# Fewer accumulating DMAs for the weighted values, two new ones for the second half's products, and another split of the last output tiles

## The chip, the cores and the metric

The kernel runs on one core of a Trainium2 chip. The metric is the device time of one execution in microseconds: the median of three runs was 166.25 us, between 166.01 and 166.59.

## What is computed

Two branches read the same input of 2048 tokens by 512 channels (bfloat16), and a gate for each token mixes them. The first is an attention of 32 heads of 16 channels, in which a token sees itself and seven earlier tokens at a distance of 2, 4, ... 14. The second is an MLP over the tokens: the normalised input is multiplied by w1 (2048 x 1792), passed through a gelu and multiplied by w2 (1792 x 2048).

```
g = sigmoid((x * gate_w).sum(-1))
logits[s, w] = (q[s] . k[s - 2 w]) / 4          # w = 0..7, masked where s - 2w < 0
o[s] = sum over w of softmax(logits)[s, w] * v[s - 2 w]
a = o @ wo
b = (w2^T gelu(w1^T layernorm(x) + b1) + b2)    # over the token axis
out = g * a + (1 - g) * b
```

## The kernel before

**Stages on TensorE.** The projections to q, k and v (L667, up to 50.4 us) come first. The MLP's first product, `ph2`, has 14 blocks of 128 hidden units (L582; 16 matmuls each, and 14 for the first four blocks, whose first two input tiles are done early at L591). Then comes the second product, `ph3`, for 16 output tiles of 128 tokens (L855; 14 matmuls of 512 columns each, in two halves). To each tile's sums the attention's projection `wo` is added in the same PSUM bank (L864; four matmuls). `wo` of a tile runs five tiles behind its `ph3`, and the last five tiles' `wo` come at the end, together with that of tile 15, which is cut into pieces by columns.

**The attention's logits.** Channels are laid out so that a group of four channels of each head ("head-dim" `dl` = 0..3) forms one layer of 128 partitions. For a half `h` of 1024 tokens VectorE multiplies q and the eight shifted copies of k, one layer at a time (`qk`, L755 to 761; 128x8192 elements for all eight distances), and adds the four products (`qadd`, L763). Buffers P0, P1 and P2 hold 128x8192 bfloat16 each; a fourth lies over the logits' space. TensorE then sums the channels of each head with 16 matmuls of 32 columns (`sum0`, `sum1`, L747), ScalarE copies the logits out (`lev`), and VectorE and ScalarE do the softmax (L784 to 799): maxima, subtraction, `exp`, three sums (`sm4`, `sm2`, `sm1`), a logarithm (`lns`), an addition (`rsz`), an exponential (`rb`) and a multiplication (`nrm`). ScalarE loads another function table between these and the gelus that stand among them in its order.

In the first half the product of layer 1 is added to that of layer 0 by an accumulating DMA that GpSimd issues (`qd0`, L769, 2 MB). In the second half VectorE does all: `qk(0)`, then for layers 1 to 3 a product into P1 and an addition to P0.

**Weighted values.** GpSimd copies the weights to all four layers (`av0_*`, `av1_*`, L809, 16 DMAs of 128 KB for each half). For each of eight units `u` of 256 tokens VectorE multiplies the weights with v (`avm`, L820, 128x8192), and the eight distances are added in three steps: 8 to 4, 4 to 2 (`avb`) and 2 to 1 (`avc`, which writes what `wo` of tiles 2u and 2u+1 reads). The first step is an accumulating DMA of 1 MB on GpSimd's queue (`avd`, L823) for the units in the list `AVD` (L30: 1 to 6) and a VectorE addition of 128x4096 (`ava`, L827) for units 0 and 7.

**The end.** ScalarE scales a finished tile from PSUM to SBUF (`ev`, L875) and SP writes it out (`d_out`, L877). Tile 15 is cut at columns 256 and 384 (L896): VectorE evacuates the first and the last piece (L911), ScalarE the second; SP writes VectorE's two, ScalarE's queue its own.

**Order.** Each operation is recorded with its engine, an assumed duration, a priority and the names of the buffers that it reads and writes (`_Sched.add`). A list scheduler (L125 to 222) gives each engine a fixed order by assumed times; semaphore waits are then planned from the buffer names (L224). Thus an edit in one place can move instructions of any engine. On TensorE most of the order is chained by hand (`PE`, L550), and the two `sum` operations are put in by priority. SP issues the loads in its own fixed order: weights of `ph2` come in seven loads `w1_0` to `w1_6` of two blocks each (three buffers; a load waits until the blocks that used its buffer are done), the weights of `ph3` in eight loads `w2_0` to `w2_7`, which reuse space of other buffers: `w2_2` goes into P2 and waits until P2 is free (`W2ALIAS`, L368).

`PR` (L370) gives the resource names of the four product buffers.

```
        PR = [["p0"], ["p1"], ["p2", "p2h"], ["log0", "log1", "att0", "att1", "lw"]]
```

Of the kernel before, what the change touches and what calls it, by code (L numbers as in the profile page):

```python
# [8 lines left out]
ALU = mybir.AluOpType  # L9
AF = mybir.ActivationFunctionType  # L10
# [3 lines left out]
D = 512  # L14
# [4 lines left out]
NST = S // 128  # L19
NFT = F // 128  # L20
PAD = 14
HS = S // 2
KR = HS + PAD
# [3 lines left out]
ZMAX = 60.0  # L27
NOELIDE = False
NLEAD = 2
AVD = (1, 2, 3, 4, 5, 6)  # L30
GL = 4


# [272 lines left out]
def bass_gated_mix__sliding_local_dilated__mixer_token_mlp__prompt_kernel(nc, A_x, A_wqkv, A_wo, B_x, B_w1, B_b1, B_w2, B_b2, gate_w, out, dbg=None):  # L306
    with contextlib.ExitStack() as es:
# [45 lines left out]
        outv = out[0].rearrange("(t p) d -> p t d", p=128)  # L353
# [7 lines left out]
        def w2view(name, extra=0):  # L361
# [5 lines left out]
               w2view("X"), w2view("X", NFT * 256)]  # L367
        W2ALIAS = [XTALL, XTALL, ["p2"], ["w1s1"], ["w1s2"], ["w1s0"],  # L368
                   ["x%d" % t for t in range(7)], ["x%d" % t for t in range(7, 14)]]
        PR = [["p0"], ["p1"], ["p2", "p2h"], ["log0", "log1", "att0", "att1", "lw"]]  # L370
        LW = view("LOG", BF16, [(128 * GL, NLEAD), (1, 128 * GL)])
        WO = view("WO", BF16, [(D, 4), (1, D)])
        QH = [view("Q%d" % h, BF16, [(HS, 4), (1, HS)]) for h in range(2)]
        KH = [view("K%d" % h, BF16, [(KR, 4), (1, KR)]) for h in range(2)]
        V5 = view("V5", BF16, [(VR, 4), (1, VR)])
        PB = [view(b, BF16, [(HS, NW), (1, HS)]) for b in ("P0", "P1", "P2", "LOG")]
# [4 lines left out]
        OT = view("OT", BF16, [(4 * UT_, 8), (UT_, 4), (1, UT_)])  # L381
        OTRES = ["log0", "log0", "log1", "log1", "att0", "att0", "att1", "att1"]
# [10 lines left out]
        OUTS = view("OUTS", BF16, [(D, 5), (1, D)])  # L393
# [32 lines left out]
        OMG = small(NST)  # L426
        C2 = small(NST)
# [4 lines left out]
        def col(v_, i):  # L432
            return bass.AP(v_.tensor, v_.offset + i, [list(v_.ap[0]), [1, 1]])
# [4 lines left out]
        def sub(ap_, offs, dims):  # L438
            return bass.AP(ap_.tensor, ap_.offset + offs, [list(ap_.ap[0])] + [list(d) for d in dims])
# [5 lines left out]
        def tt(o_, a_, b_, op_):  # L445
            return lambda e: e.tensor_tensor(out=o_, in0=a_, in1=b_, op=op_)  # L446

        def act(o_, i_, f_, **kw):
            return lambda e: e.activation(out=o_, in_=i_, func=f_, **kw)  # L449
# [170 lines left out]
        r0 = rstd(0)  # L620
# [5 lines left out]
        r1 = rstd(1)  # L626
# [65 lines left out]
        for dl in range(4):  # L692
# [3 lines left out]
          reads=["k%d_1" % dl for dl in range(4)], writes=["khalo"], name="khalo")  # L696
# [8 lines left out]
        for dl in range(4):  # L705
            for sb in range(4):
                proj(2, dl, sb)
            if dl == 0:
                te = bank_()

                def f_te(e):
# [6 lines left out]
                  reads=["b%d" % te], writes=["e1"], name="e1", prio=-30)  # L718
# [4 lines left out]
        for t in range(NLEAD, NST):  # L723
            A("dve", (lambda t_: lambda e: e.bn_stats(out=ST6[:, t_, :], in_=X[:, t_, :]))(t), 0.67,  # L724
              reads=["x%d" % t], writes=["st%d" % t], after=[e3], name="st%d" % t, prio=-4)
# [28 lines left out]
        for h in range(2):  # L754
            def qk(dl, b_):  # L755
                for s_, n_ in (((0, 512), (512, 512)) if h == 0 else ((0, HS),)):
                    sbs = [2 * h + x_ for x_ in range(s_ // 512, (s_ + n_) // 512)]
                    A("dve", tt(sub(PB[b_], s_, [(HS, NW), (1, n_)]), sub(QH[h], dl * HS + s_, [(0, NW), (1, n_)]),
                                sub(KH[h], dl * KR + PAD + s_, [(-2, NW), (1, n_)]), ALU.mult), 4.32 * n_ / HS + 0.1,
                      reads=["q%d_%d" % (dl, x_) for x_ in sbs] + ["k%d_%d" % (dl, x_) for x_ in sbs] + (["khalo"] if h else ["kpad"] if s_ == 0 else ["k%d_0" % dl]),  # L760
                      writes=PR[b_], name="qk%d_%d_%d" % (h, dl, s_))

            def qadd(a_, b_):  # L763
                A("dve", tt(PB[a_], PB[a_], PB[b_], ALU.add), 4.42, reads=PR[b_], writes=PR[a_], name="qa%d_%d" % (h, a_))
            if h == 0:
                qk(0, 0)
                qk(1, 1)
                rows = [(2048, 4), (1, 2048)]
                sch.dma("pool", (lambda d_, s_: lambda e: e.dma_start(d_, s_, accum_op=ALU.add, max_dma_last_dim=4096))(sub(PB[0], 0, rows), sub(PB[1], 0, rows)),  # L769
                        int(3.2e6), sch.dsem("qd%d" % h), issue=1.0, reads=PR[1], writes=PR[0], name="qd%d" % h)  # L770
                qk(2, 2)
                qk(3, 3)
                qadd(2, 3)
                qadd(2, 0)
                fin = 2
            else:
                qk(0, 0)
                for dl in range(1, 4):
                    qk(dl, 1)
                    qadd(0, 1)  # L780
                fin = 0
            A("pe", f_sum(fin), 1.0, reads=PR[fin] + ["rp"], writes=LGB, name="sum%d" % h, prio=-100, delay=0.5)
            A("act", act(LOG[h], ps[:, 4:8, :], AF.Copy), 1.9, reads=LGB, writes=["log%d" % h], name="lev%d" % h, prio=-5)
            if h == 0:  # L784
# [30 lines left out]
        for u in range(8):  # L815
            h, c = u // 4, u % 4
            b = 1 if u % 2 == 0 else 0
            pv = PV[b]
            vr = ["v%d_%d" % (dl, sb) for dl in range(4) for sb in sorted(set([u // 2, max(0, (256 * u - PAD)) // 512]))]
            A("dve", tt(pv, sub(V5, PAD + 256 * u, [(-2, NW), (VR, 4), (1, UT_)]), sub(AVW[h], c * NW * UT_, [(UT_, NW), (0, 4), (1, UT_)]), ALU.mult), 4.42,  # L820
              reads=["avw%d_%d_%d" % (h, c, dhi) for dhi in range(4)] + vr + ["vpad"], writes=["p%d" % b], name="avm%d" % u)
            if u in AVD:
                sch.dma("pool", (lambda d_, s_: lambda e: e.dma_start(d_, s_, accum_op=ALU.add, max_dma_last_dim=4096))(  # L823
                    sub(PB[b], 0, [(2048, 2), (1, 2048)]), sub(PB[b], 4096, [(2048, 2), (1, 2048)])),
                    int(1.6e6), sch.dsem("avd%d" % u), issue=1.0, writes=["p%d" % b], name="avd%d" % u)
            else:
                A("dve", tt(pv[:, 0:4], pv[:, 0:4], pv[:, 4:8], ALU.add), 2.28, writes=["p%d" % b], name="ava%d" % u)  # L827
            A("dve", tt(pv[:, 0:2], pv[:, 0:2], pv[:, 2:4], ALU.add), 1.22, writes=["p%d" % b], name="avb%d" % u)
            avl = A("dve", tt(OT[:, u], pv[:, 0], pv[:, 1], ALU.add), 0.68, reads=["p%d" % b], writes=["ot%d" % u, OTRES[u]], name="avc%d" % u)


        ring[0], ring[1] = 0, [0, 1, 2, 3]
# [34 lines left out]
            return fn  # L867

        ds_out = [sch.dsem("out%d" % k_) for k_ in range(4)]
        ds_last = [sch.dsem("outl%d" % k_) for k_ in range(3)]  # L870

        def finish_tile(i):
            bank = banks[i]
            PE(f_wo(i, bank, 0, D), 0.87, ["ot%d" % (i // 2), "wo"], ["b%d" % bank], "wo%d" % i)
            A("act", act(OUTS[:, i % 4, :], ps[:, bank, :], AF.Identity, scale=col(OMG, i), bias=col(C2, i)), 0.78,  # L875
              reads=["b%d" % bank, "omg", "c2"], writes=["outs%d" % (i % 4)] + (["p2h"] if i == 0 else []), name="ev%d" % i)
# [13 lines left out]
        for i in range(3, L):  # L890
            ph3(i, 0)
            ph3(i, 1)
            if i >= LAG:
                finish_tile(i - LAG)
        lastb = [bank_(), bank_(), bank_()]
        CH = ((0, 256), (256, 384), (384, 512))  # L896
        for hf, (c0, c1) in enumerate(CH):
            for half in range(2):
                PE(f_ph3(L, lastb[hf], half, c0, c1), 1.52 * (c1 - c0) / D, ["ut%d" % ft for ft in range(7 * half, 7 * half + 7)] + ["w2_%d" % (L // 2)],
# [3 lines left out]
        for hf, (c0, c1) in enumerate(CH):  # L903
            bank = lastb[hf]
            n_ = c1 - c0
            PE(f_wo(L, bank, c0, c1), 0.87 * n_ / D, ["ot%d" % (L // 2), "wo"], ["b%d" % bank], "wo%d_%d" % (L, hf))
            if hf == 1:
                A("act", act(OUTS[:, 4, c0:c1], ps[:, bank, 0:n_], AF.Identity, scale=col(OMG, L), bias=col(C2, L)), 0.4,
                  reads=["b%d" % bank, "omg", "c2"], writes=["outl%d" % hf], name="ev%d_%d" % (L, hf))
            else:  # L910
                A("dve", (lambda bank_, a_, b_: lambda e: e.tensor_scalar(out=OUTS[:, 4, a_:b_], in0=ps[:, bank_, 0:b_ - a_], scalar1=col(OMG, L),  # L911
                                                                          scalar2=col(C2, L), op0=ALU.mult, op1=ALU.add))(bank, c0, c1), 0.55 if hf == 0 else 0.4,
                  reads=["b%d" % bank, "omg", "c2"], writes=["outl%d" % hf], name="ev%d_%d" % (L, hf))
            sch.dma("act" if hf == 1 else "sp", (lambda a_, b_: lambda e: e.dma_start(outv[:, L, a_:b_], OUTS[:, 4, a_:b_]))(c0, c1), 256 * n_,
                    ds_last[hf], issue=0.5, reads=["outl%d" % hf], name="d_out%d_%d" % (L, hf))

        est = sch.schedule()
# [73 lines left out]
```

## Time and profile before

| | us |
|---|---|
| median of three runs | 166.25 (166.01 to 166.59) |
| the profiled execution | 165.4 |
| its span, first to last instruction | 164.1 |
| TensorE busy | 160.7 |
| VectorE busy | 143.1 |
| ScalarE busy | 77.0 |
| GpSimd busy | 26.8 |

The profile is of one execution. Its times are in microseconds from the start of the span, and lines such as L855 are those of the kernel. "PE" is TensorE, "DVE" VectorE, "ACT" ScalarE, "POOL" GpSimd and "SP" the engine that issues most DMAs; a "q" behind the name is the issue of a DMA. The granted TensorE clock was full throughout. Queue q1 holds the DMAs that SP issues, q0 those of GpSimd. A share of DMA engines over 100% comes from packets that overlap.

### The profile page before, as it was taken

What the parts mean: (1) busy time and instruction counts of PE and PEld (TensorE: products, weight loads), DVE (VectorE), ACT (ScalarE), POOL (GpSimd) and SP (SyncE); (2) the same over time, 40 slices, a digit from 0 to 9 for tenths busy, and PEclk for the clock granted to TensorE, in tenths of its full rate; (3) what the DMA queues carried; (4) which work ended last, traced back from release to release, by engine and by line L of the source; (5) the groups of instructions that cost most, each with busy time, mean ns of one, the idle gap of its engine ahead of it and who ended that gap; (6) DMA issues with size and microseconds to landing.
All of it is one profiled execution on the core that took longest, in us unless ns stands there. A gap on an engine that the chain in (4) does not pass through costs nothing.

```text
span 164.1 us, 2044 instructions
## 1 busy us (share of the span) xinstructions
PE 160.7 (98%) x819; PEld 76.8 (47%) x819; DVE 143.1 (87%) x113; ACT 77.0 (47%) x108; POOL 26.8 (16%) x61
## 2 busy tenths in 40 slices
PE   7999999999999999999999999999999999999994
PEld 3455555545554444444444444444444444444742
DVE  2939999999999999999999999999749294699992
ACT  3466776777776639849211977100121111111164
POOL 3000030000000000000693003087270302002000
PEclk9999999999999999999999999999999999999999
DMA  5999999999503899844898869999999997956914
GB/s 168 301 261 249 242 321 279 212 215 274 175 0 110 237 327 282 228 142 115 235 261 256 279 187 270 269 213 371 227 238 211 210 204 162 213 136 115 207 60 131
DMA packets 45150, 35.26 MB, mean 215 GB/s; under 512 B 7893, under 2 KB 41941, under 8 KB 45141
## 3 DMA queue, kind: packets, MB, share of 16 engines
q1 hardware_dynamic: 40960, 22.25, 49.9%
q0 software_dynamic: 3696, 12.59, 36.0%
q10 hardware_dynamic: 484, 0.30, 0.6%
q8 instruction: 6, 0.10, 0.2%
q14 instruction: 4, 0.02, 0.0%
HBM read 18.88 MB, written 2.10 MB: 128 GB/s over the span
## 4 chain that ended last, share of the span: by engine, by line
PE 95%; DMA 2%; DVE 1%; SPq 0%; issue 0%
PE ps L855 29%; PE ps L582 29%; PE ps L667 25%; PE ps L864 8%; DMA arena<-in_A_x_dram 2%; PE ps L747 1%; PE ps L591 1%; PE ps L684 1%; DVE arena L911 1%; SPq L483 0%; PE ps L559 0%; PE ps L714 0%; PE ps L574 0%; PE ps L576 0%; PE ps L575 0%
## 5 line engine op out<-in xcount | busy, mean ns | idle before, releaser
L446 DVE TENSOR_TENSOR arena<-arena 128x8192 bf16<-128x8192 bf16 (+9 forms) x67 | 125.4, 1905 | 14.1 <-DMA arena<-arena 10.1
L449 ACT ACTIVATE arena<-ps,arena 128x512 bf16<-128x512 f32 (+1 forms) x30 | 21.6, 725 | 61.1 <-PE ps L864 45.0
L855 PE MATMUL ps<-arena 128*128 128x512 bf16 (+2 forms) x252 | 50.2, 355 | 0.0
L582 PE MATMUL ps<-arena 128*128 128x512 bf16 x216 | 47.1, 379 | 0.0
L449 ACT ACTIVATE arena<-ps 128x512 bf16<-128x512 f32 (+3 forms) x53 | 34.2, 645 | 16.8 <-PE ps L667 14.0
L667 PE MATMUL ps<-arena 128*128 128x512 bf16 x192 | 42.0, 379 | 0.0
L855 PEld LDWEIGHTS ps<-arena 128*128 128x128 bf16 x252 | 23.6, 98 | 25.2
L582 PEld LDWEIGHTS ps<-arena 128*128 128x128 bf16 x216 | 21.0, 98 | 25.8 <-issue 0.8
L667 PEld LDWEIGHTS ps<-arena 128*128 128x128 bf16 x192 | 21.6, 113 | 19.7 <-ACT arena L449 0.4
L809 POOL DMA_DIRECT2D arena<-arena x32 | 17.6, 678 | 61.9 <-DVE arena L446 61.9
L864 PE MATMUL ps<-arena 128*128 128x512 bf16 (+2 forms) x72 | 15.8, 356 | 0.0
L940 ACT ACT_TABLE_LOAD x11 | 14.1, 1283 | 2.9 <-issue 2.7
L823 POOL DMA_DIRECT2D arena<-arena x6 | 7.3, 1220 | 39.6 <-DVE arena L446 39.6
L864 PEld LDWEIGHTS ps<-arena 128*128 128x128 bf16 x72 | 6.6, 98 | 7.5 <-DVE arena L446 0.8
L449 ACT ACTIVATE arena<-arena 128x1 f32<-128x1 f32 (+6 forms) x14 | 7.6, 544 | 4.2 <-DVE arena L446 3.6
L724 DVE BATCH_NORM_STATS2 arena<-arena 128x6 f32<-128x512 bf16 x14 | 8.7, 681 | 0.0
L769 POOL DMA_DIRECT2D arena<-arena x1 | 1.4, 1421 | 19.8 <-DVE arena L446 19.8
L737 DVE TENSOR_SCALAR arena<-arena 128x512 bf16<-128x512 bf16 x14 | 4.6, 407 | 0.0
L544 PE MATMUL ps<-const-bfloat16-1.0 128*128 128x512 bf16 x8 | 3.5, 569 | 0.9 <-PEq L976 0.9
L596 DVE BATCH_NORM_STATS2 arena<-arena 128x6 f32<-128x512 bf16 x2 | 1.4, 694 | 1.6 <-DMA arena<-in_A_x_dram 1.6
L911 DVE TENSOR_SCALAR arena<-ps,arena 128x256 bf16<-128x256 f32 (+1 forms) x2 | 0.9, 473 | 1.6 <-PE ps L864 1.6
L747 PE MATMUL ps<-arena 128*32 128x512 bf16 x32 | 2.1, 382 | 0.0
(37 smaller groups left out, 15.9 us busy)
## 6 DMA issues: line engine op xcount, KB each, us to landing
arena<-in_B_w_dram SPq DMA_DIRECT2D x10, 896.0 KB, 6.7
arena<-arena POOLq DMA_DIRECT2D x6, 1024.0 KB, 10.2
arena<-in_B_w_dram SPq DMA_DIRECT2D x5, 1024.0 KB, 6.8
arena<-arena POOLq DMA_DIRECT2D x32, 128.0 KB, 6.1
arena<-arena POOLq DMA_DIRECT2D x1, 2048.0 KB, 17.8
out_dram<-arena SPq DMA_DIRECT2D x15, 128.0 KB, 4.5
arena<-in_A_wqkv_dram SPq DMA_DIRECT2D x3, 512.0 KB, 5.8
arena<-in_A_x_dram SPq DMA_DIRECT2D x3, 512.0 KB, 4.8
```

The costliest lines, as they stand in the source:

```text
L446: return lambda e: e.tensor_tensor(out=o_, in0=a_, in1=b_, op=op_)
L449: return lambda e: e.activation(out=o_, in_=i_, func=f_, **kw)
L582: ins = e.matmul(ps[:, bank, :], lhsT=W1W[:, (ft // 2) % 3, st, 128 * (ft % 2):128 * (ft % 2) + 128], rhs=X[:, st, :], start=(st == 0), st ...
L667: ins = e.matmul(ps[:, bank, :], lhsT=sub(WQKV, dt * 3 * D + tn * D + dl, [(4, 128)]), rhs=XT[:, dt, sb * 512:(sb + 1) * 512], start=(dt = ...
L724: A("dve", (lambda t_: lambda e: e.bn_stats(out=ST6[:, t_, :], in_=X[:, t_, :]))(t), 0.67, reads=["x%d" % t], writes=["st%d" % t], after=[ ...
L737: A("dve", (lambda t_: lambda e: e.tensor_scalar(out=X[:, t_, :], in0=X[:, t_, :], scalar1=col(MS, t_), scalar2=col(RSTD2, t_), op0=ALU.su ...
L747: ins = e.matmul(ps[32 * c:32 * c + 32, 4 + wp, :], lhsT=RP, rhs=sub(PB[b_], 2 * wp * HS + c * UT_, [(HS, 2), (1, UT_)]), start=True, stop ...
L809: prev = sch.dma("pool", (lambda d_, s_: lambda e: e.dma_start(d_, s_))(dst, src), 131072, ds, issue=1.0, reads=["att%d" % h], writes=["av ...
L823: sch.dma("pool", (lambda d_, s_: lambda e: e.dma_start(d_, s_, accum_op=ALU.add, max_dma_last_dim=4096))(sub(PB[b], 0, [(2048, 2), (1, 20 ...
L855: ins = e.matmul(ps[:, bank, 0:c1 - c0], lhsT=W2S[i // 2][:, ft, 128 * (i % 2):128 * (i % 2) + 128], rhs=UT[:, ft, c0:c1], start=(ft == 0) ...
L864: ins = e.matmul(ps[:, bank, 0:c1 - c0], lhsT=OT[:, i // 2, dl, 128 * (i % 2):128 * (i % 2) + 128], rhs=WO[:, dl, c0:c1], start=False, sto ...
L940: e.preload_act_table_set(want)
```

## The change

It has four parts in the source.

1. `AVD` becomes 1, 3, 5: in units 2, 4 and 6 VectorE does the first addition.
2. In the second half, layers 0 and 1 are multiplied in two halves of four distances each (`qkw`, 128x4096), into P0 and P1; after each half of layer 1 a DMA of 1 MB (`qd1_0`, `qd1_4`) adds P1's half to P0's. Layer 2 is multiplied into P2, layer 3, again in two halves, into P1 as its halves come free, then P1 and P0 are added to P2. The sum is now in P2. P0 and P1 have two resource names each, one for each half.
3. Tile 14 is evacuated by VectorE.
4. Tile 15 is cut into two pieces, at column 288: the first is evacuated by ScalarE and written by its queue, the second by VectorE and SP.

```diff
-AVD = (1, 2, 3, 4, 5, 6)
+AVD = (1, 3, 5)
...
-        PR = [["p0"], ["p1"], ["p2", "p2h"], ["log0", "log1", "att0", "att1", "lw"]]
+        PR = [["p0", "p0b"], ["p1", "p1b"], ["p2", "p2h"], ["log0", "log1", "att0", "att1", "lw"]]
...
+            def qkw(dl, b_, w0):
+                A("dve", tt(sub(PB[b_], w0 * HS, [(HS, 4), (1, HS)]), sub(QH[h], dl * HS, [(0, 4), (1, HS)]),
+                            sub(KH[h], dl * KR + PAD - 2 * w0, [(-2, 4), (1, HS)]), ALU.mult), 2.25,
+                  reads=["%s%d_%d" % (c_, dl, 2 * h + x_) for c_ in "qk" for x_ in range(2)] + ["khalo"],
+                  writes=PR[b_][w0 // 4:w0 // 4 + 1], name="qk%d_%d_w%d" % (h, dl, w0))
...
+            def qd(b0, n_, nm, nb):
+                rows = [(2048, n_), (1, 2048)]
+                r0, r1 = (PR[0], PR[1]) if n_ == 4 else (PR[0][b0:b0 + 1], PR[1][b0:b0 + 1])
+                sch.dma("pool", (lambda d_, s_: lambda e: e.dma_start(d_, s_, accum_op=ALU.add, max_dma_last_dim=4096))(sub(PB[0], 4096 * b0, rows), sub(PB[1], 4096 * b0, rows)),
+                        nb, sch.dsem(nm), issue=1.0, reads=r1, writes=r0, name=nm)
...
             else:
-                qk(0, 0)
-                for dl in range(1, 4):
-                    qk(dl, 1)
-                    qadd(0, 1)
-                fin = 0
+                for w0 in (0, 4):
+                    qkw(0, 0, w0)
+                    qkw(1, 1, w0)
+                    qd(w0 // 4, 2, "qd1_%d" % w0, int(2.2e6))
+                qk(2, 2)
+                qkw(3, 1, 0)
+                qkw(3, 1, 4)
+                qadd(2, 1)
+            qadd(2, 0)
+            fin = 2
...
+        def ev_dve(i, o, bank, c0, c1, dur, res):
+            A("dve", lambda e: e.tensor_scalar(out=OUTS[:, o, c0:c1], in0=ps[:, bank, 0:c1 - c0], scalar1=col(OMG, i), scalar2=col(C2, i),
+                                               op0=ALU.mult, op1=ALU.add), dur, reads=["b%d" % bank, "omg", "c2"], writes=[res], name="ev%d_%d" % (i, c0))
...
+            if i == NST - 2:
+                ev_dve(i, i % 4, bank, 0, D, 0.75, "outs%d" % (i % 4))
+            else:
...
-        lastb = [bank_(), bank_(), bank_()]
-        CH = ((0, 256), (256, 384), (384, 512))
+        lastb = [bank_(), bank_()]
+        CH = ((0, 288), (288, 512))
```

The order that the scheduler then makes differs in these places. On TensorE `sum1` stands 16 matmuls of `ph2` earlier. On VectorE the second half's three half products come before the first half's softmax, the fourth after `msub0`; unit 1 is multiplied before unit 0, and unit 3 before unit 2. On SP `w2_2`, whose space is P2, is issued after `sum1` and not after `sum0`, behind `w2_3`. On ScalarE `lns1` comes before the last gelu.

More of the change, by code (lines that the diff above doesn't have):

```diff
@@ L767, in bass_gated_mix__sliding_local_dilated__mixer_token_mlp__prompt_kernel @@
                 qk(1, 1)
-                rows = [(2048, 4), (1, 2048)]
-                sch.dma("pool", (lambda d_, s_: lambda e: e.dma_start(d_, s_, accum_op=ALU.add, max_dma_last_dim=4096))(sub(PB[0], 0, rows), sub(PB[1], 0, rows)),
-                        int(3.2e6), sch.dsem("qd%d" % h), issue=1.0, reads=PR[1], writes=PR[0], name="qd%d" % h)
+                qd(0, 4, "qd0", int(3.2e6))
                 qk(2, 2)
@@ L773, in bass_gated_mix__sliding_local_dilated__mixer_token_mlp__prompt_kernel @@
                 qadd(2, 3)
-                qadd(2, 0)
-                fin = 2
-            else:
-                qk(0, 0)
-                for dl in range(1, 4):
-                    qk(dl, 1)
-                    qadd(0, 1)
-                fin = 0
+            else:
+                for w0 in (0, 4):
[8 more added lines that the diff above has]
+            fin = 2
             A("pe", f_sum(fin), 1.0, reads=PR[fin] + ["rp"], writes=LGB, name="sum%d" % h, prio=-100, delay=0.5)
@@ L820, in bass_gated_mix__sliding_local_dilated__mixer_token_mlp__prompt_kernel @@
             A("dve", tt(pv, sub(V5, PAD + 256 * u, [(-2, NW), (VR, 4), (1, UT_)]), sub(AVW[h], c * NW * UT_, [(UT_, NW), (0, 4), (1, UT_)]), ALU.mult), 4.42,
-              reads=["avw%d_%d_%d" % (h, c, dhi) for dhi in range(4)] + vr + ["vpad"], writes=["p%d" % b], name="avm%d" % u)
+              reads=["avw%d_%d_%d" % (h, c, dhi) for dhi in range(4)] + vr + ["vpad"], writes=PR[b], name="avm%d" % u)
             if u in AVD:
@@ L824, in bass_gated_mix__sliding_local_dilated__mixer_token_mlp__prompt_kernel @@
                     sub(PB[b], 0, [(2048, 2), (1, 2048)]), sub(PB[b], 4096, [(2048, 2), (1, 2048)])),
-                    int(1.6e6), sch.dsem("avd%d" % u), issue=1.0, writes=["p%d" % b], name="avd%d" % u)
+                    int(1.6e6), sch.dsem("avd%d" % u), issue=1.0, writes=PR[b], name="avd%d" % u)
             else:
-                A("dve", tt(pv[:, 0:4], pv[:, 0:4], pv[:, 4:8], ALU.add), 2.28, writes=["p%d" % b], name="ava%d" % u)
-            A("dve", tt(pv[:, 0:2], pv[:, 0:2], pv[:, 2:4], ALU.add), 1.22, writes=["p%d" % b], name="avb%d" % u)
-            avl = A("dve", tt(OT[:, u], pv[:, 0], pv[:, 1], ALU.add), 0.68, reads=["p%d" % b], writes=["ot%d" % u, OTRES[u]], name="avc%d" % u)
+                A("dve", tt(pv[:, 0:4], pv[:, 0:4], pv[:, 4:8], ALU.add), 2.28, writes=PR[b], name="ava%d" % u)
+            A("dve", tt(pv[:, 0:2], pv[:, 0:2], pv[:, 2:4], ALU.add), 1.22, writes=PR[b], name="avb%d" % u)
+            avl = A("dve", tt(OT[:, u], pv[:, 0], pv[:, 1], ALU.add), 0.68, reads=PR[b], writes=["ot%d" % u, OTRES[u]], name="avc%d" % u)
         ring[0], ring[1] = 0, [0, 1, 2, 3]
@@ L869, in bass_gated_mix__sliding_local_dilated__mixer_token_mlp__prompt_kernel @@
         ds_out = [sch.dsem("out%d" % k_) for k_ in range(4)]
-        ds_last = [sch.dsem("outl%d" % k_) for k_ in range(3)]
+        ds_last = [sch.dsem("outl%d" % k_) for k_ in range(2)]
+        def ev_dve(i, o, bank, c0, c1, dur, res):
+            A("dve", lambda e: e.tensor_scalar(out=OUTS[:, o, c0:c1], in0=ps[:, bank, 0:c1 - c0], scalar1=col(OMG, i), scalar2=col(C2, i),
+                                               op0=ALU.mult, op1=ALU.add), dur, reads=["b%d" % bank, "omg", "c2"], writes=[res], name="ev%d_%d" % (i, c0))
         def finish_tile(i):
@@ L874, in finish_tile @@
             PE(f_wo(i, bank, 0, D), 0.87, ["ot%d" % (i // 2), "wo"], ["b%d" % bank], "wo%d" % i)
-            A("act", act(OUTS[:, i % 4, :], ps[:, bank, :], AF.Identity, scale=col(OMG, i), bias=col(C2, i)), 0.78,
-              reads=["b%d" % bank, "omg", "c2"], writes=["outs%d" % (i % 4)] + (["p2h"] if i == 0 else []), name="ev%d" % i)
+            if i == NST - 2:
+                ev_dve(i, i % 4, bank, 0, D, 0.75, "outs%d" % (i % 4))
+            else:
+                A("act", act(OUTS[:, i % 4, :], ps[:, bank, :], AF.Identity, scale=col(OMG, i), bias=col(C2, i)), 0.78,
+                  reads=["b%d" % bank, "omg", "c2"], writes=["outs%d" % (i % 4)] + (["p2h"] if i == 0 else []), name="ev%d" % i)
             sch.dma("sp", (lambda i_: lambda e: e.dma_start(outv[:, i_, :], OUTS[:, i_ % 4, :]))(i), 131072, ds_out[i % 4], issue=0.5,
@@ L906, in bass_gated_mix__sliding_local_dilated__mixer_token_mlp__prompt_kernel @@
             PE(f_wo(L, bank, c0, c1), 0.87 * n_ / D, ["ot%d" % (L // 2), "wo"], ["b%d" % bank], "wo%d_%d" % (L, hf))
-            if hf == 1:
+            if hf == 0:
                 A("act", act(OUTS[:, 4, c0:c1], ps[:, bank, 0:n_], AF.Identity, scale=col(OMG, L), bias=col(C2, L)), 0.4,
-                  reads=["b%d" % bank, "omg", "c2"], writes=["outl%d" % hf], name="ev%d_%d" % (L, hf))
+                  reads=["b%d" % bank, "omg", "c2"], writes=["outl%d" % hf], name="ev%d_%d" % (L, c0))
             else:
[L911 to L914, printed above, removed]
+                ev_dve(L, 4, bank, c0, c1, 0.5, "outl%d" % hf)
+            sch.dma("act" if hf == 0 else "sp", (lambda a_, b_: lambda e: e.dma_start(outv[:, L, a_:b_], OUTS[:, 4, a_:b_]))(c0, c1), 256 * n_,
                     ds_last[hf], issue=0.5, reads=["outl%d" % hf], name="d_out%d_%d" % (L, hf))
```

## The prediction

> **What bounds the kernel now.** I read the page's first part, then the chain of work that ended last, then the waits, then the DMA by queue in short windows. TensorE is nearly the whole span:
>
> ```profile
> PE 160.7 (98%) x819; PEld 76.8 (47%) x819; DVE 143.1 (87%) x113; ACT 77.0 (47%) x108; POOL 26.8 (16%) x61
> ```
>
> The chain in order of time (start, us, what) is matmuls to the end, and VectorE only in the last microsecond:
>
> ```profile
> 53.47 0.98 PE ps L747 x16
> 54.45 35.07 PE ps L582 x162
> 89.52 0.98 PE ps L747 x16
> ...
> 156.28 4.98 PE ps L864 x24
> 161.26 0.03 issue
> 161.29 0.86 DVE arena L911 x2
> ```
>
> So a step matters if it makes TensorE wait, lets it wait less, or shortens what follows its last matmul. 162 matmuls of L582 in 35.07 us are 0.2165 us each. From 54.45 on, the only matmuls of 512 columns that start more than 0.25 us after the one before them, other than at L747, are two in the tail: wo12 0.07 us late and wo14 0.12 us late, for VectorE (avc6 ends at 157.86, avc7 at 159.72). VectorE's three waits for accumulating DMAs (3.20, 3.16 and 3.72 us, 10.1 in all) cost TensorE those 0.19 us and nothing else.
>
> **Part 1, weighted values.** avd2, avd4 and avd6 go and three VectorE additions of 128x4096 come, at 2.29 us each (the row of ten), 2.20 from start to start. 3 x 2.20 = 6.6 us of work against 10.1 us of waits. With part 2, which starts this chain 2.2 us earlier, avc7 ends near 159.7 - 10.1 + 6.6 - 2.2 = 154.0; TensorE wants it at 159.6. Some 5 us to spare, so a DMA a few us late is covered. Value: the 0.19 us.
>
> **Part 2, second half's products.** VectorE before: four products and three additions of 128x8192, 7 x 4.42. After: six halves at 2.29, one product and two additions at 4.42: 27.0 against 30.9 us. The scheduler therefore moves sum1 (L747, second run) 16 matmuls earlier on TensorE, to 89.52 - 16 x 0.2165 = 86.06. Does VectorE make that? From 50.64 (the first product): three halves at 2.20, then mask and maxima, 2.88 as before, to 60.12; a half to 62.32; product 2 to 66.66; the three sums, 2.32, to 68.98; the half that waits for qd1_0, to 71.18; rsz. Then nrm0 waits for ScalarE: lns0 at 69.11 as before, then a table load 1.28, gelu 0.69, load 1.28 and rb0 0.42, so 73.25. nrm0 starts at 73.30; the half that waits for qd1_4 at 74.44, the additions at 76.76 and 81.22, the last ending at 85.64. That is 0.4 us ahead of TensorE: free, but no more than that.
>
> The two DMAs are the question. GpSimd issues 0.31 us after VectorE ends (111.71 to 112.02 at avd2): qd1_0 at 55.44, qd1_4 at 62.72. VectorE needs them at 68.98 and 74.44, 13.5 and 11.7 us later. The six 1 MB adds of before took 7.8 to 13 us, median 10.2, so they nearly fit. But they do something to the other queue. Here is the DMA by queue (packets, MB, share of 16 engines) for 29 to 38 us, while qd0 runs:
>
> ```profile
> q0 software_dynamic: 419, 1.72, 95.3%
> q1 hardware_dynamic: 412, 0.21, 11.4%
> ```
>
> The adds (q0, packets of 4096 bytes at 327 ns) and SP's loads (q1, packets of 512 bytes) go one for one, so the loads fall from some 300 GB/s to 23. w1_1, issued at 18.96, landed only at 39.41. A 1 MB add is 256 packets, 16 per engine: 16 x 0.327 = 5.2 us in which the weights of the MLP nearly stand still. In before no add runs between 40 and 80 us; in after two run between 57 and 74, where TensorE eats w1 loads as they come. w1_3 is the first wanted: ph2_6 starts after three groups of 14 and two of 16 matmuls from 54.38, at 70.36. Before, it landed at 65.90, 4.5 us early.
>
> When would it land? w2_2 leaves this window (its buffer, P2, now holds the second half's sum, so it waits for sum1). w2_1 is issued at 55.45, first packets 1.07 later as with w2_2; a load from its first packets to landing is 3.63 (w2_2), a w1 load behind another 3.59 (62.31 to 65.90). So 56.52 + 3.63 + 3.59 = 63.74 without adds, and 63.74 + 5.23 = 68.97 with qd1_0 in front. That is 1.4 us early. With qd1_4 also in front it is 68.97 + 5.23 = 74.2, or 3.8 us late. All hangs on whether qd1_4 starts before w1_3 is through. An add in an idle stretch has its first packet 1.76 us after issue (147.65 to 149.41). In a busy one it takes much longer (GpSimd's timeline, and the DMA from 101.1 to 104.9 and 105 to 106):
>
> ```profile
> 21.93 1.42 POOL L769 DMA_DIRECT2D arena<-arena  x1 [19.85 <-DVE arena L446]
> 99.83 1.23 POOL L823 DMA_DIRECT2D arena<-arena  x1 [12.19 <-DVE arena L446]
> ```
>
> ```profile
> q1 hardware_dynamic: 2167, 1.10, 119.4%
> ```
>
> ```profile
> q0 software_dynamic: 54, 0.22, 110.6%
> q1 hardware_dynamic: 66, 0.03, 12.0%
> ```
>
> avd1, issued at 99.83, moves nothing until 104.99 (5.16 us), qd0 nothing until 27.58 (5.65): loads already queued go ahead. For qd1_4 this gives 62.72 + 5.16 = 67.88 to 68.37. w1_3's last packets are some 0.3 us before its landing, at 68.67. So 0.3 to 0.8 us of it, at 36 packets per us and engine some 11 to 29 packets on each engine, are still to come, and each of the first 16 costs a whole pair, 0.36 us. Bounds: none left, no wait; 16 or more left, landing at 74.2. I take 12 left, near the lower of the two rows, since qd1_4 is the shape of avd1: 68.1 + 12 x 0.36 + 0.3 = 72.7, **TensorE 2.4 us late** at ph2_6 (both ends, 0 and 3.8, stay in the range). Later loads then are no trouble: w1_4, wanted at 77.27, comes at the latest 3.6 us after w1_3, near 77.8, by when TensorE is itself 2.4 to 3.8 us late.
>
> [...]
>
> **What else moves.** Behind the two new waits of VectorE stand rsz0, nrm0 and the additions; nrm0 in turn is what GpSimd's first 16 copies of weights (av0) wait for, now at 74.5 (before 79.1), behind qd1_4 on the same queue. Copies landed a median 6.1 us after issue; the first unit that reads them starts at 85.7, so some 11 us are there. On SP, w2_2 moves behind three w1 loads and w2_3, to sum1's end near 87; ph3_4 wants it near 111, and such loads took 5 to 16 us. On ScalarE gel13 moves behind lns1, with a table load between: VectorE's third sum ends near 99.4, so lns1 99.9, load 1.28, gelu 0.69: 101.9, where ph3_0's second half wants it at 103.8. All three cost nothing with these margins, and with 2 us lost from the last one the loss would go to TensorE in full.
>
> **Part 3, the tail.** Before, SP issues d_out14 at 161.66, then two pieces of tile 15 at 162.03 and 162.51; the last lands at 164.09, 1.58 after issue, and the span ends. After, SP has one piece of tile 15, ScalarE's queue the other. TensorE is 0.19 earlier, and perhaps 0.04 more for fewer narrow matmuls: wo14 at 159.55, its result at 160.59. VectorE takes tile 14: 0.54 for 256 columns and 0.40 for 128 give 0.83 for 512 by extension: 161.46. The 224 columns need TensorE until 161.44, then 0.51: 161.99. Issue at 162.02, landing 1.58 to 1.7 later, 163.6 to 163.7. The end is **0.42 us earlier** (0.35 to 0.5). The ScalarE piece (288 columns, 0.59) is issued at 161.72 and lands before that. Where VectorE at 512 columns took 1 us, SP's last issue would slip 0.2.
>
> **Sum.** In the profiled execution (165.4 us, span 164.1): 165.4 - 0.4 + 2.4 = 167.4. It lies 0.85 below the median of the runs shown, 166.25: 168.2 there.
>
> **Rivals.**
> - *The loads get by.* qd1_4 starts 0.5 us later than I took, or w1_3 a little sooner, and w1_3 lands before 70.36. This decides at one point: w1_3 landed, or not, when TensorE reaches ph2_6. Then w1_4 is next: qd1_4 in front puts it near 77.1 against 77.27, just in time. Time: 166.25 - 0.4 = 165.8. For it: 1.4 us of margin behind one add, and queued loads go ahead. If the runs without a profile (0.85 us longer) lose more than 0.19 to VectorE's waits in the tail, more comes back, down to 165.1. **Not slower, some faster.** Chance 0.41.
> - *sum1 becomes the wait.* VectorE has 0.4 us of margin, behind a chain of table loads and qd1_4. If qd1_4 lands 1 to 2 us after 74.44 (an add of before took up to 13 us from issue, which would be 75.7), sum1 is late by 0.6 to 1.6 with w1_3 in time: 166.25 - 0.4 + 1 = 166.9. Chance 0.07.
> - *It doesn't do what it says.* The adds that stay might land no sooner and VectorE still wait; with 5 us to spare that changes nothing at the end, so it has no time of its own.
> - *Forecast*, w1_3 late at ph2_6 by 0.9 to 3.8 us: 166.8 to 169.7, likeliest 168.2. Chance 0.52.
>
> **Numbers.** The measurement tells 0.3% (0.5 us) from no change. Of the 0.41, 0.27 is under 165.75 and 0.14 within; 0.06 of the other cases is within: faster 0.27, same 0.20, slower 0.53. Range for 8 in 10: from 165.3, low in the first rival, to 169.6, nearly both ends of the wait; the forecast's own is 166.8 to 169.7.
>
> **What would show it.** Right: a gap before the L582 matmul number 89 near 70.4, released by the load's DMA; w1_3 landing after 70.4; q1 at some 11% while q0 is at 95% between 58 and 74; w2_2 issued after sum1; no wait of TensorE for VectorE in the tail; 0.4 us less after the last wo matmul together with its earlier start. Wrong: L582 as one piece up to sum1 at 86.1 (the loads got by), or a gap at L747 instead (sum1). If the time falls by more than 1.2 us, I have missed something that held TensorE.

## The result, and the profile after

| | before | after |
|---|---|---|
| median, same chip, six runs each | 166.39 us (165.98 to 167.92) | 173.20 us (172.56 to 173.87) |
| the profiled execution | 165.4 | 173.41 |
| its span | 164.1 | 172.2 |

The change makes the kernel slower: the ratio of times is 1.040 (95% interval 1.035 to 1.045), above the top of the predicted range.

These are rows of the page of the profile after: busy time, the clock granted to TensorE in 40 slices, the group of L582, and two rows of the DMA issues (the last column is the median from issue to landing).

```profile
PE 163.5 (95%) x801; PEld 77.2 (45%) x801; DVE 146.4 (85%) x118; ACT 79.1 (46%) x109; POOL 25.4 (15%) x60
...
PEclk9999999999999999965999999999999999999999
...
L582 PE MATMUL ps<-arena 128*128 128x512 bf16 x216 | 49.4, 391 | 5.5 <-DMA arena<-in_B_w_dram 5.5
...
arena<-in_B_w_dram SPq DMA_DIRECT2D x5, 1024.0 KB, 15.8
arena<-arena POOLq DMA_DIRECT2D x5, 1024.0 KB, 9.1
```

TensorE fell from 98% of the span to 95%, although it has 18 narrow matmuls fewer to do (tile 15 is in two pieces and not three). L582 has one wait of 5.5 us, for a load of weights. Two slices of the clock row, the 18th and 19th (73.2 to 81.8 us), are at 0.6 and 0.5, where the row of before is full throughout. The median load of 1 MB takes 15.8 us to land; in before it was 6.8:

```profile
arena<-in_B_w_dram SPq DMA_DIRECT2D x5, 1024.0 KB, 6.8
```

The chain that ended last, in order of time (start, us, what):

```profile
54.23 0.98 PE ps L747 x16
55.21 3.14 PE ps L582 x14
58.35 0.02 issue
58.36 18.27 DMA arena<-in_B_w_dram
76.64 0.14 issue
76.78 17.85 PE ps L582 x72
94.62 0.98 PE ps L747 x16
...
164.81 5.21 PE ps L876 x28
170.01 0.03 issue
170.04 0.51 DVE arena L885
```

In before this was one piece of L582 from `sum0` to `sum1`. Now a transfer stands in it: `w1_3`, issued at 58.36, lands at 76.64, and the next matmul starts 0.14 us later. All of TensorE's work before 58.36 was done in time; what follows is late by what this load is late. Everything here is 0.76 us later than in the profile of before from the start on (`sum0` at 54.23 and 53.47; the first load of the input took 0.7 us longer). Nothing that the change moves stands ahead of that, so 0.76 is taken off in what follows where a time is said to be on before's footing.

What TensorE did around it, in stretches (from:to, length; busy us and number of instructions of PE, PEld, DVE, ACT, POOL; granted clock; DMA share; GB/s):

```profile
69.00:71.00 2.00, 2.00 (x11) 0.84 (x9) 1.97 (x3) 1.96 (x3) 0.00 (x0) 1.00 1.05 211
71.00:76.70 5.70, 0.28 (x2) 0.00 (x0) 3.79 (x4) 4.27 (x5) 1.12 (x3) 0.79 1.08 254
76.70:81.30 4.60, 4.53 (x12) 1.61 (x13) 4.57 (x2) 0.00 (x0) 4.60 (x10) 0.52 1.18 300
81.30:85.00 3.70, 3.70 (x19) 1.70 (x18) 3.67 (x2) 0.69 (x1) 2.50 (x5) 1.00 1.07 375
```

Two losses can be read here. TensorE idles from 71.1 to 76.78. Then, for 4.6 us, it is busy but gets 12 matmuls done where the last row has 19 in 3.7 us: in the trace nine matmuls start 0.427 us after the one before them, one 0.379 and one 0.300, instead of 0.216. The granted clock is 0.5 from 74.33 to 81.16. That is 9 x 0.211 + 0.16 + 0.08 = 2.15 us.

Who kept the DMA engines busy is seen in two windows of the DMA by queue (packets, MB, share of 16 engines). Between the two adds, 66.9 to 68.5:

```profile
q1 hardware_dynamic: 1041, 0.53, 113.5%
q8 instruction: 1, 0.02, 4.6%
```

During the second add, 68.7 to 74:

```profile
q0 software_dynamic: 240, 0.98, 92.7%
q1 hardware_dynamic: 355, 0.18, 15.6%
```

The loads' queue gets 1041 packets through in 1.6 us, and then 355 in 5.3 us: a tenth of the rate. (The one packet of q8 holds 16 KB of instructions; it comes up again below.)

**The sum.** The wait: from 71.12 (0.216 after the last matmul's start) to 76.78, 5.65 us. The slow matmuls: 2.15. The later start: 0.76. The tail is shorter by 0.52 (worked out below). 5.65 + 2.15 + 0.76 - 0.52 = 8.04 us, and 172.17 - 164.13 = 8.04. The medians differ by less, 6.8 us; the starts of the runs without a profile are not known.

### The profile page after: what moved, and what is told of

Same layout as the page of the kernel before. It is cut to its first block, busy times and chain, and to the rows that moved or that the text cites. A ratio compares the mean times of both kernels' runs of the same rounds, so it can differ in the third digit from the quotient of the medians.

```text
span 172.2 us, 2011 instructions
## 1 busy us (share of the span) xinstructions
PE 163.5 (95%) x801; PEld 77.2 (45%) x801; DVE 146.4 (85%) x118; ACT 79.1 (46%) x109; POOL 25.4 (15%) x60
## 4 chain that ended last, share of the span: by engine, by line
PE 85%; DMA 13%; SPq 0%; DVE 0%; issue 0%
PE ps L867 28%; PE ps L667 24%; PE ps L582 21%; DMA arena<-in_B_w_dram 11%; PE ps L876 8%; DMA arena<-in_A_x_dram 2%; PE ps L747 1%; PE ps L591 1%; PE ps L684 1%; SPq L483 0%; PE ps L559 0%; DVE arena L885 0%; PE ps L714 0%; PE ps L574 0%; PE ps L576 0%
## 5 line engine op out<-in xcount | busy, mean ns | idle before, releaser
L446 DVE TENSOR_TENSOR arena<-arena 128x2048 bf16<-128x2048 bf16 (+9 forms) x72 | 128.1, 1813 | 13.1 <-ACT arena L449 11.7
L582 PE MATMUL ps<-arena 128*128 128x512 bf16 x216 | 49.4, 391 | 5.5 <-DMA arena<-in_B_w_dram 5.5
L449 ACT ACTIVATE arena<-ps,arena 128x512 bf16<-128x512 f32 (+1 forms) x29 | 21.1, 727 | 68.6 <-PE ps L876 47.4
L667 PE MATMUL ps<-arena 128*128 128x512 bf16 x192 | 42.0, 379 | 0.0
L582 PEld LDWEIGHTS ps<-arena 128*128 128x128 bf16 x216 | 21.4, 100 | 33.2 <-issue 9.7
L867 PEld LDWEIGHTS ps<-arena 128*128 128x128 bf16 x238 | 23.3, 98 | 25.4
L667 PEld LDWEIGHTS ps<-arena 128*128 128x128 bf16 x192 | 21.6, 113 | 19.7 <-ACT arena L449 0.4
L821 POOL DMA_DIRECT2D arena<-arena x32 | 17.0, 643 | 30.9 <-DVE arena L446 30.9
L774 POOL DMA_DIRECT2D arena<-arena x3 | 3.8, 1273 | 58.8 <-DVE arena L446 58.8
L876 PEld LDWEIGHTS ps<-arena 128*128 128x128 bf16 x68 | 6.6, 98 | 7.2
L885 DVE TENSOR_SCALAR arena<-ps,arena 128x512 bf16<-128x512 f32 (+1 forms) x2 | 1.3, 660 | 7.4 <-PE ps L876 7.3
L835 POOL DMA_DIRECT2D arena<-arena x3 | 3.7, 1230 | 24.5 <-DVE arena L446 24.5
L544 PE MATMUL ps<-const-bfloat16-1.0 128*128 128x512 bf16 x8 | 4.0, 628 | 0.8 <-PEq L993 0.8
L559 PEld LDWEIGHTS ps<-arena 128*128 128x128 bf16 x16 | 1.3, 125 | 2.1 <-DMA arena<-in_A_x_dram 1.3
## 6 DMA issues: line engine op xcount, KB each, us to landing
arena<-in_B_w_dram SPq DMA_DIRECT2D x5, 1024.0 KB, 15.8
```

Of the source, the lines that this page charges most:

```text
L544: ins = e.matmul(ps[:, bank, :], lhsT=WONE, rhs=WROW, start=True, stop=True)
L582: ins = e.matmul(ps[:, bank, :], lhsT=W1W[:, (ft // 2) % 3, st, 128 * (ft % 2):128 * (ft % 2) + 128], rhs=X[:, st, :], start=(st == 0), st ...
L667: ins = e.matmul(ps[:, bank, :], lhsT=sub(WQKV, dt * 3 * D + tn * D + dl, [(4, 128)]), rhs=XT[:, dt, sb * 512:(sb + 1) * 512], start=(dt = ...
L821: prev = sch.dma("pool", (lambda d_, s_: lambda e: e.dma_start(d_, s_))(dst, src), 131072, ds, issue=1.0, reads=["att%d" % h], writes=["av ...
L867: ins = e.matmul(ps[:, bank, 0:c1 - c0], lhsT=W2S[i // 2][:, ft, 128 * (i % 2):128 * (i % 2) + 128], rhs=UT[:, ft, c0:c1], start=(ft == 0) ...
L876: ins = e.matmul(ps[:, bank, 0:c1 - c0], lhsT=OT[:, i // 2, dl, 128 * (i % 2):128 * (i % 2) + 128], rhs=WO[:, dl, c0:c1], start=False, sto ...
```

## The experiments

The theory after the result: the two adds of part 2 starve `w1_3`, since the loads get one packet through for each of an add's (47 and 47 in after, 71 to 72 us) and this load stands too far back; and part of the loss is not the wait but TensorE's clock after it. The rivals: the loss comes from elsewhere in the change; one add is as bad as two; it is the bytes that the adds move in all, wherever the load stands; the slow matmuls come from the DMAs running beside them and not from the idleness.

Each ratio is against the kernel before, run on the same chip beside it (medians 166.25 in the first set, experiments 1, 3, 4 and 5, and 166.45 in the second, experiments 2, 6 and 7).

### 1. The change without part 2

Weighted values and the tail as in after, the second half's products as in before:

```diff
-                for w0 in (0, 4):
-                    qkw(0, 0, w0)
-                    qkw(1, 1, w0)
-                    qd(w0 // 4, 2, "qd1_%d" % w0, int(2.2e6))
-                qk(2, 2)
...
+                qk(0, 0)
+                for dl in range(1, 4):
+                    qk(dl, 1)
+                    qadd(0, 1)
```

> Parts 1, 3 and 4 alone: the second half's logits are made as before the change (no qd1 adds, w2_2 back after sum0). Theory S (the whole loss is part 2: its two accumulating DMAs hold back w1_3, and the wait then costs TensorE clock): no TensorE wait in L582, and the tail gains forecast for parts 1, 3 and 4, so 0.4 us less than before, 166.0 us. Rival P (parts 1, 3, 4 cost something too, by longer VectorE work in front of wo or a later last write): 166.4 us or more.

Measured: 165.87 us (165.27 to 167.6, 12 runs), ratio 0.9988 [0.9954, 1.0022]. TensorE's timeline (start, us, what) has the products in one piece again:

```profile
55.44 35.14 PE L582 MATMUL ps<-arena 128*128 128x512 bf16 x159
90.50 1.05 PE L747 MATMUL ps<-arena 128*32 128x512 bf16 x16
```

No matmul of the tail waits for VectorE. So parts 1, 3 and 4 cost nothing that can be measured. Whether they gain the forecast 0.4 us the times can't tell: the median agrees, the interval holds no change as well. This is the only version with a median below that of the kernel before, and it can't be told from it.

### 2. Part 2 alone

The kernel before with part 2 of the diff and nothing else.

> Before with part 2 of the change alone (the second half's products with the two adds); weighted values and the tail as before. Theory S (part 2 is the whole loss): a wait of 5 to 6 us in L582 at ph2_6 and ten slow matmuls after it, as in the changed kernel; VectorE's two short waits in the tail are gone since TensorE is late, so 173.2 to 173.6 us. Rival P (parts 1, 3 and 4 carry some of the loss): under 172.5 us.

Measured: 173.14 us (171.43 to 174.9, six runs), ratio 1.0405 [1.0348, 1.0462], as after. Its profile is of its longest run, but the two stretches around the wait read as those of after:

```profile
72.00:77.40 5.40, 0.34 (x1) 0.00 (x0) 3.19 (x4) 4.33 (x5) 0.76 (x2) 0.86 1.08 253
77.40:82.00 4.60, 4.51 (x11) 1.61 (x12) 4.57 (x2) 0.00 (x0) 4.60 (x10) 0.50 1.16 298
```

Part 2 is the whole loss, wait and slow clock both.

### 3. TensorE kept busy during the wait

After with 26 matmuls on constants, into a spare bank, ahead of `ph2_6`. They are no part of the reference's computation and change no output.

```diff
+            if ft == 6:
+                PE(f_warm(26, 4), 0.0, [], [], "fill")
```

> The changed kernel with 26 matmuls on constants (an unused PSUM bank, 5.6 us) put on TensorE ahead of ph2_6, where it waited 5.87 us for w1_3. Nothing else is changed, so w1_3 lands as late. Theory C (the ten matmuls at 427 ns after the wait come from the idle time before them): those matmuls run at 0.216 us, and the time falls by about 2.1 us from 173.2 to 171.1. Rival (they are slow because of what they read, or the idle time is not the cause): they stay at 427 ns and the time stays at 173.2.

Measured: 171.89 us (171.21 to 172.09, four runs), ratio 1.0326 [1.0268, 1.0385]. In stretches, the constant matmuls and what follows:

```profile
71.70:77.40 5.70, 5.70 (x27) 2.58 (x26) 3.74 (x4) 4.24 (x5) 1.14 (x3) 1.00 1.08 255
77.40:82.00 4.60, 4.60 (x23) 2.06 (x21) 4.57 (x2) 0.69 (x1) 4.60 (x10) 1.00 1.17 299
```

`w1_3` is as late as in after (it lands from 75.63 to 77.01 on its 16 DMA engines), but the matmuls behind it now follow every 0.216 us: 23 recorded in 4.6 us against 12. (The clock column says nothing here: this trace holds no record of the clock, and the view then prints 1.00.) With the start taken off (this profile starts 0.67 us later than after's) the span is 172.17 - (170.73 - 0.67) = 2.1 us shorter; the medians, from which no start can be taken off, differ by 1.3 us. The slow matmuls are thus a cost of their own, caused by the idleness and not by the DMAs, which run as in after.

### 4. Only the first add by DMA

The second half is added by VectorE (128x4096).

```diff
-                    qd(w0 // 4, 2, "qd1_%d" % w0, int(2.2e6))
+                    if w0 == 0:
+                        qd(0, 2, "qd1_0", int(2.2e6))
+                    else:
+                        A("dve", tt(sub(PB[0], 4096, [(1, 4096)]), sub(PB[0], 4096, [(1, 4096)]), sub(PB[1], 4096, [(1, 4096)]), ALU.add), 2.28,
+                          reads=["p1b"], writes=["p0b"], name="qh1")
```

> The changed kernel with the second of the two adds (qd1_4) done by VectorE (one more 128x4096 addition); qd1_0 stays an accumulating DMA. Theory S: w1_3 stands behind one add only. With qd1_0 ending near 66.8 and 1816 packets of w1_3 left at 690 a us it lands at 69.4 to 71.0, before TensorE wants it at 71.1: no wait, 165.9 to 166.4 us. Rival D (any add between 56 and 75 delays w1_3 by its own length, the loss goes by the bytes): half the wait, some 2.9 us, 169 us.

Measured: 166.40 us (165.68 to 168.65, 12 runs), ratio 1.0012 [0.9983, 1.0041]. The chain:

```profile
58.53 13.12 DMA arena<-in_B_w_dram
71.65 0.14 issue
71.79 10.52 PE ps L582 x48
```

`w1_3` lands between 69.83 and 71.65 (15 of its 16 engines by 70.19), and TensorE is 0.5 us late. The wait for the load nearly goes with the second add, and `sum1` is on time although VectorE has 2.3 us more work. The second add's place behind the first is what hurts.

### 5. `w2_1` behind `w1_4`

SP's order: `w2_1`, which nobody wants before `ph3`, is moved from ahead of `w1_3` to behind `w1_4`.

```diff
-            ld_w2(j)
+            o_ = ld_w2(j)
+            if j == 1:
+                o_.order.add(w1op[4])
```

> The changed kernel with both adds; SP issues w2_1 behind w1_4 instead of ahead of w1_3. Theory S (what counts is how much of SP's queue stands unfinished when qd1_4 starts): w1_3 is now first in the queue; it shares 16 packets per engine with qd1_0 and is through at about 66 to 67, before or just as qd1_4 starts; TensorE waits 0 to 1.5 us, 165.9 to 167.5 us. Rival D (the loss goes by the bytes moved before w1_3): the adds' 10.5 us stay and only w2_1's 3 us go, so about 2.9 us of wait are left, and 169 to 170 us.

Measured: 173.24 us (172.82 to 174.98, six runs), ratio 1.0438 [1.0386, 1.0489]: neither forecast. The wait at `ph2_6` is gone, and another has come. The chain:

```profile
71.41 2.31 PE ps L584 x10
73.73 17.71 DMA arena<-in_B_w_dram
91.44 0.14 issue
91.58 3.57 PE ps L584 x8
```

`w1_3` was in time (68.32 to 69.48). But SP's instruction that issues `w2_1` took from 65.41 to 73.68, 8.27 us instead of 0.37. It ended as the second add's last packets went (from 67.88 on, 95% of them by 73.35), but the trace doesn't say what it waited for. SP could issue `w1_5` only behind it, at 73.73, and that load, behind `w2_1` and beside GpSimd's copies of the weights, landed at 91.44. TensorE waits 5.4 us for it and runs slow afterwards, as in after (granted clock 0.50 from 91.5 to 97). The wait was moved from `w1_3` to `w1_5`.

### 6. `w2_1` behind `w1_6`

As above with `w1op[6]`: no load of `ph3` stands ahead of any load that `ph2` wants. Both adds stay.

> The changed kernel with both adds; SP issues w2_1 only behind w1_6, so that none of the four w1 loads stands behind it. Theory Q (a load is late when what stands ahead of it in SP's queue, together with the adds, has not moved by the time TensorE wants it; in the run with w2_1 behind w1_4 the wait moved to ph2_10, whose w1_5 stood behind w2_1): no wait at ph2_6, ph2_8 and ph2_10 over 1 us, 165.9 to 167 us. Rival B (the two adds fill the engines so far that some w1 load is late in any order): a wait of 2 us or more somewhere in L582 before sum1, 168.5 us or more.

Measured: 166.84 us (165.4 to 167.68, 12 runs), ratio 1.0016 [0.9981, 1.0051]. TensorE's timeline (this profile starts 1.4 us later than after's):

```profile
56.55 31.95 PE L584 MATMUL ps<-arena 128*128 128x512 bf16 x143
88.44 1.05 PE L749 MATMUL ps<-arena 128*32 128x512 bf16 x16
```

One piece again; the largest gap in it is 0.27 us. The same adds move the same bytes in about the same time (6.6 and 7.3 us from first to last packet, 6.1 and 6.6 in after) and cost nothing that can be measured, once 0.9 MB that nobody waits for are out of the way. So it is not the adds' traffic as such that costs, but what it leaves for the load that TensorE wants next. The gain is not only that `w1_3` has less ahead of it: with no load moving, the first add has its first packet 1.76 us after its issue and not 4.83, so it is over sooner, and the loads have the engines to themselves for 3.2 us between the adds (1.7 in after).

### 7. The adds in packets of 512 bytes

```diff
-            def qd(b0, n_, nm, nb):
+            def qd(b0, n_, nm, nb, ml=4096):
...
-                    qd(w0 // 4, 2, "qd1_%d" % w0, int(2.2e6))
+                    qd(w0 // 4, 2, "qd1_%d" % w0, int(2.2e6), 512)
```

Inside `qd`, `max_dma_last_dim=ml`.

> The changed kernel with the two adds cut into packets of 512 bytes, the size of the loads' packets, in place of 4096. Theory T (the engines take turns between the two queues a packet at a time): while an add runs the loads get about half the packets and some 100 GB/s or more in place of 23, w1_3 lands earlier than 75.9 after the same start, and the wait at ph2_6 shrinks by 2 us or more; the adds take longer, so VectorE is late and sum1 (L747) waits instead. Rival G (an add has precedence over loads as a whole, whatever its packets): the loads stay near 23 GB/s or below while it runs, and the wait at ph2_6 is 5 us or more.

Measured: 174.02 us (172.94 to 177.87, four runs), ratio 1.0435 [1.0368, 1.0502]. The DMA by queue from 62 to 69, while both queues have work:

```profile
q0 software_dynamic: 1378, 0.71, 78.7%
q1 hardware_dynamic: 1378, 0.71, 49.2%
```

Exactly as many packets of the one as of the other. With equal packets the loads get half of the bytes, 101 GB/s instead of 23. So while both queues moved they went packet for packet, with packets of one size here as with 4096 and 512 bytes (47 and 47 in after, 71 to 72 us). The waits of this kernel (us in total, times, longest):

```profile
DVE arena L446 <- DMA arena<-arena: 8.3, 2, 6.0
...
PE ps L582 <- DMA arena<-in_B_w_dram: 5.6, 2, 3.0
```

The wait at `ph2_6` is half as long, but the adds now take 10 and 11 us instead of 6.1 and 6.6. They hold back `w1_4` as well (a second wait, 3.0 us in this view, at 82) and VectorE, which waits for both of them. `sum1`, which had been expected to wait for VectorE, doesn't. Equal shares did not help here, where there was too much to move by the time it was wanted: L582 still waits 5.6 us in all.

## Why the prediction was right and wrong

**Right: the sign, the place and the mechanism.** TensorE waits at `ph2_6`, matmul 89, for `w1_3`, behind the two adds, while q1 has 11 to 16% of the engines. GpSimd issued the adds where forecast (55.44 and 62.72, plus 0.76):

```profile
56.21 1.18 POOL L774 DMA_DIRECT2D arena<-arena  x1 [32.06 <-DVE arena L446]
63.48 1.19 POOL L774 DMA_DIRECT2D arena<-arena  x1 [6.09 <-DVE arena L446]
```

The second add's first packet came at 68.54, so 67.78 on before's footing, 5.06 us after its issue, where 67.88 to 68.37 was taken. Experiments 2, 4 and 6 show the cause: part 2 alone brings the loss, one add does not, and both do not if the load stands further ahead.

**Right: the other terms.** In the waits of after, VectorE's 10.1 us for accumulating DMAs are down to 0.2, and its waits for ScalarE are up from 2.8 to 11.7:

```profile
DVE arena L446 <- ACT arena L449: 11.7, 4, 6.4
...
DVE arena L446 <- DMA arena<-arena: 0.2, 1, 0.2
```

The 0.2 is for the second half add, that lands at 75.49. No matmul of `wo12` and `wo14` waits, 0.19 us as forecast; from the start of `wo14`'s last matmul to the end are 3.43 us (before 3.70), and the matmuls from `sum1` to there take 0.06 less besides, so the tail brings 0.52, a little more than the 0.42 (0.35 to 0.5). VectorE's sum of the second half ends at 86.73 - 0.76 = 85.97 (forecast 85.64), just ahead of the 86.06 at which TensorE was to want it, so `sum1` would have been on time; that rival falls, and experiments 4 and 6 show `sum1` on time. The 6.4 us that VectorE now waits is for ScalarE's copies of the logits, which wait for the late `sum1`.

**Wrong, first term: the packets that were left.** The step that failed is "I take 12 left", and with it the wait of 2.4 us. When the second add starts, the trace has 728 packets of `w1_3` to go, 45 or 46 on each engine, and the wait was 5.65 us. Three things lie in the difference.

- *The 12 does not follow from the prediction's own rows.* It means to go by `avd1`, whose first packet came 5.16 us after issue. That gives a start at 67.88, 0.79 us ahead of the last packets, so 29 left by its own count: 16 full turns, a landing at 74.2 and a wait of 3.8 us. 12 left belongs to a start at 68.34, as late as `qd0`'s. The start came at 67.78, for which the same count gives 32.
- *The load was behind its sum.* In experiment 4, with one add, 15 of the 16 engines had landed `w1_3` by 70.19, that is 69.26 on before's footing, where the sum had 68.97. `w2_1`, which stands ahead of it, still had 245 of its 1792 packets to go at the first add's first packet (61.04), so this add ran almost wholly ahead of `w1_3`, which got most of its packets only in the 1.7 us between the adds.
- *The load's slowest engine was behind the others.* In after 15 of 16 completions of `w1_3` come by 75.55, the last at 76.64, and the next matmul starts at 76.78; in experiment 4 the last comes 1.46 us behind the others, and it alone makes the load late there. The trace has a possible reason, no more than the author's estimate: the packet of q8, 16 KB of instructions, which takes 1.18 us from 68.20 on (1.15 us from 68.70 in experiment 4). Each of the nine traces has such a packet between 65 and 71 us. The first `w1` load that lands after its end has its last completion 0.9 to 1.5 us behind the 15th in all nine (0.87 in before, 1.09 in after, 1.46 in experiment 4); the loads that land between 55 us and its end have theirs within 0.4. No run takes the packet away, so this is not shown by an experiment.

With 45 the sum closes: 67.78, then 16 turns of 0.36 is 5.8, then 29 packets at 36 per us is 0.8, then 0.3 to landing, gives 74.7, and 1.1 for the slowest engine 75.8; measured 76.64 - 0.76 = 75.88. The prediction's upper bound, 74.2, left out the last engine and took 5.2 for the 16 turns, the add's packets without the load's between them. So its range was too narrow even for the mechanism that it had right.

The prediction gives "loads already queued go ahead" as the reason for an add's late start. The delay had the right size, the reason is not shown: the first add of after was issued at 56.21, 0.24 us ahead of `w2_1` and with no load moving until 57.48, and `w2_1` still went ahead of it.

**Wrong, second term: not foreseen.** The clock. The prediction costed a wait at its length. After 5.65 us of idleness some ten matmuls took double, 2.15 us more; experiment 3 gives 1.3 us by medians and 2.1 by profiles. The profile of before had a row with which to price it: the eight matmuls of L544 at its beginning, where nothing has run yet, have 569 ns each, and in the trace the first ones start 0.427 us apart.

```profile
L544 PE MATMUL ps<-const-bfloat16-1.0 128*128 128x512 bf16 x8 | 3.5, 569 | 0.9 <-PEq L976 0.9
```

The granted clock reads as full there (1.00 from 0.8 to 3.4 us), but this trace's records of the clock begin only at 3.90 us, so only the spacing shows it.

In the seven traces that hold records of the clock, its changes lie whole multiples of 3.41 us apart: in after the record starts at 6.07 us and changes at 74.33 and 81.16, 20 and 2 times 3.413 us on. The half clock lasted 6.83 us in after (74.33 to 81.16) and 3.41 in experiment 7 (73.94 to 77.35). In experiment 7 the wait of 2.8 us at 71 (from one matmul's start to the next, less 0.216) cost clock, and that of 3.1 us at 82 none. So the length of a wait alone did not decide what it cost; what did is not shown.

**What the sum should have been.** On the profile before: 165.4 - 0.52 + 5.65 + 2.15 = 172.7; measured 173.41 - 0.76 = 172.65.

## What to carry to other kernels

An addition that is given to the DMA engines frees the engine that does it (2.3 us of VectorE for 128x4096 here), and was paid for here by a wait for a load: `w1_3` in after, `w1_5` in experiment 5. For each load that the bounding engine wants next, count all that stands ahead of it on its own queue, add one of the other queue's packets for every packet of its own (0.36 us a pair here), up to as many as the add has (16 on an engine here), add what its slowest engine is behind the others (0.9 to 1.5 us here), and ask whether a load that nobody wants yet can go behind it: here that one move took back the whole loss, while moving it only half way moved the wait. A wait of some microseconds on TensorE is to be costed with the slow matmuls that can follow it, here 2.15 us after a wait of 5.65.

## What the runs showed of the hardware

- **A transfer's first packet came late while the other queue moved**: an add's 4.83 and 5.06 us after issue in after, 5.16 and 5.65 in before, against 1.76 with no load moving (before at 147.65, experiments 5 and 6). A load's did too: in experiment 6 `w1_3` was issued at 59.78, while the first add moved, and had its first packet at 64.92. What decides it is not shown: in experiment 7 an add issued at 98.19 beside loads began after 1.80 us.
- **An issue held its engine.** SP's instruction took 0.37 us for ten of the twelve loads issued after 50 us in before, but 5.07 us for `w1_5` in after, 8.27 for `w2_1` in experiment 5 and 13.5 at 26.10 in before, beside the first half's add; what SP had to issue next waited.
- **In smaller packets the adds were slower**: in packets of 4096 bytes (327 ns) an add beside loads had 190 GB/s (before, 29 to 38 us), in 512 (64 ns) 101 GB/s (experiment 7, 62 to 69 us), and GpSimd's issue took 2.1 us instead of 1.2.
- **TensorE's clock** after a wait: matmuls at half speed for 4.4 us after 5.65 us (after), for 3.4 us after 2.8 us (experiment 7), and no loss after 3.1 us (experiment 7) or 0.5 us (experiment 4). Its changes lay whole multiples of 3.41 us apart.
- **One packet of instructions** (16 KB) took 1.0 to 1.2 us at 65 to 71 us in every trace (1.19 in before, 1.18 in after). `w1_3` had landed only with its last engine, 1.09 us behind the 15th in after.
